# Loading q and k with 48 rows instead of 40, the last eight zeros

## The chip, the cores and the metric

The kernel runs on one core of a Trainium2 chip. The metric is device time in microseconds of one execution; several executions are timed and the median is given. The engines of the core are TensorE (PE, with its weight loads shown as PEld), VectorE (DVE), ScalarE (ACT), GpSimd (POOL) and SyncE (SP), which here issues nearly all DMA transfers. Sixteen DMA engines carry the transfers.

## What is computed

An mLSTM recurrence over 4 batches, 8 heads and 768 tokens with a head dimension of 40, gated and normalized, and then a dense layer of 3072 tokens: 320 to 2048, softplus, 2048 to 320.

```python
for t in range(S):
    m_new = np.maximum(f_gate[:, :, t] + m, i_gate[:, :, t])
    f_stab = np.exp(f_gate[:, :, t] + m - m_new)
    i_stab = np.exp(i_gate[:, :, t] - m_new)
    C = f_stab[:, :, None, None] * C + i_stab[:, :, None, None] * np.einsum('bhd,bhe->bhde', vt, kt)
    n = f_stab[:, :, None] * n + i_stab[:, :, None] * kt
    h_tilde = np.einsum('bhde,bhe->bhd', C, qt)
    denom = np.maximum(np.abs(np.einsum('bhd,bhd->bh', n, qt)[:, :, None]), 1.0)
    y[:, :, t] = o * h_tilde / denom
x = y.transpose(0, 2, 1, 3).reshape(B * S, H * D)
h = x @ w_in
g = np.maximum(h, 0.0) + np.log1p(np.exp(-np.abs(h)))
out = g @ w_out
```

## The kernel before

The recurrence is cut into 24 steps of one batch and 128 tokens each. A step has its scores (products of k and q, 64 tokens by 64, `scores`, L463), the decay matrix that weighs them (`decay`, `by_decays`), the products of k and decayed v for the state (`states`, L480), the values (`values`, L579 and L587, or `values_wide`, L640 and L652), and then normalization, gate and transpose into a tile X (`turn_x`, L707 and L709). Three steps make a group of 384 tokens, eight groups in all. The dense layer runs group by group in 16 blocks of 128 hidden units: eight products into hp (L974), softplus, nine products into po (L937). The matmuls of the dense layer fill TensorE; the steps of later groups are worked into the gaps between the blocks. Only the first group has nothing to run beside it: its three steps, and the splitting of the first weights, come before the first product of L974.

q and k of a step are loaded by `load` (L382): one tile `qk` of 128 partitions, three buffers, with the head dimension on the partitions, 1024 floats (q and k, four heads, 128 tokens) a row. The heads come in two halves (x is 0 or 1): one half goes to the partitions from 0, the other to those from 64 (PP is 64). Each half is one transfer, issued on SP; the third transfer of `load` is `vt`, v and k by token, with 128 rows. D is 40, EP is 48. The products read rows `x * PP` to `x * PP + D` and no others.

The order of all work is written out by hand: `WHEN` gives a time for each piece, and `in_order` fixes the order of the instructions on each engine. SP's order at the start is: gates, first weights, q/k and vt of step 0, q/k and vt of step 1, output gates, q/k and vt of step 2, a write of gate values, more weights. In the first 40 us TensorE's order is: warm-up products on `po1` (L731), gate spreading, decay broadcasts of steps 0 and 1 (L396), scores of step 0, decay broadcast of step 2 (L396), scores of step 1, states of step 0, warm-up, values of step 0, warm-up, states of step 1, values of step 1, scores, states and values of step 2, the transposes, scores and states of step 3, first product. Tiles of the scores are named ga, or po for step 1, whose scores lie in spare banks; those of the values gc, or po.

Of the kernel before, what the change touches and what calls it, by code (L numbers as in the profile page):

```python
# [17 lines left out]
B, H, S, D = 4, 8, 768, 40  # L18
# [14 lines left out]
PP = 64  # L33
EP = 48
# [8 lines left out]
def mlstm_moe_kernel(  # L43
# [11 lines left out]
    nc = tc.nc  # L55
# [322 lines left out]
    def load(z):  # L378

        z.qk = p2.tile([128, 2, HG, L], F32, tag="qk", bufs=3, name=f"qk{z.n}")  # L380
        for x in range(2):
            nc.sync.dma_start(z.qk[x * PP : x * PP + D], qk[z.s, x])  # L382
        z.q, z.k = z.qk[:, 0], z.qk[:, 1]
        z.vt = p2.tile([128, VW + DM], F32, tag="vt", bufs=3, name=f"vt{z.n}")
        nc.sync.dma_start(z.vt, vk[z.s])
        z.v1 = z.vt[:, 0:VW].rearrange("p (q j e) -> p q j e", q=NQ, j=HG)
        z.kt = z.vt[:, VW:]
# [443 lines left out]
    def plain_step(z, times):  # L831
        spare = z.s in (1, 2)
        fs = dict(
            load=load, fb=decays, scan=decay, vi=gate_values, vw=state_values, sig=out_gate,
            ga=plain_scores, pm=by_decays, st=states, cp=keep_states, old=decay_old,
            mid=mid_state, new=new_state, gc=lambda z: values(z, z.s in SPARE_C), sum=sum_values, nrm=norm, sg=scale_gate, x=gated,
            xp=turn_x, xh=high_x, xl=low_x,
        )
        for (name, f), t in zip(fs.items(), times, strict=True):
            once(f"{name}{z.s}", t, event, name, f, z)  # L840
# [3 lines left out]
    def wide_step(z, base, after):  # L844
        d = 18 + 30 * (z.s == NH)
        g = after - base
        for name, f, t in (
            ("fb", decays, -64), ("load", load, -48), ("scan", decay, -8), ("vw", state_values, 2), ("old", decay_old, 6),
            ("ga", group, 14), ("pm", by_decays, 17), ("cp", keep_states, 17), ("vi", gate_values, 20), ("mid", mid_state, 24),
            ("new", new_state, 30), ("fc", load_decays, g - 34),  # L850
        ) + ((("gc", values_wide, g),) if z.s == NS - 1 else ()) + (
            ("ym", scale_wide, g + 5), ("ya", add_wide, g + 5), ("yd", write_wide, g + 8), ("rd", read_wide, g + 42),
            ("fin", finish_wide, g + 91 + d), ("end", end_wide, g + 92 + d), ("xh", high_wide, g + 95 + d),
            ("xl", low_wide, g + 98 + d),
        ):
            once(f"{name}{z.s}" if z.s < 9 else name, base + t, event, name, f, z, base=base)
# [328 lines left out]
```

## Time and profile before

| | us |
|---|---|
| median of three runs | 439.82 |
| lowest and highest | 436.81, 440.22 |
| span of the profiled execution | 438.4 |

| engine | busy us | share of the span |
|---|---|---|
| PE | 427.3 | 97% |
| DVE | 253.6 | 58% |
| ACT | 214.5 | 49% |
| POOL | 106.1 | 24% |

The profile is of one execution. Busy time of PE is that of pipelined matmuls. The granted clock is given as a share: 1.00 is 2.4 GHz, 0.50 is 1.2 GHz. The DMA share is the mean over the sixteen DMA engines. The DMAs moved 55.93 MB in the span. The chain that ended last is 95% PE and 3% DMA.

### The profile page before, as it was taken

Reading aid. Unit: us, or ns where it says so; the run is one execution under the profiler, and the core shown is the slowest. Engines: PE = TensorE matmul, PEld = TensorE weight load, DVE = VectorE, ACT = ScalarE, POOL = GpSimd, SP = SyncE. Lnnn points to the kernel's source line nnn. Section 1 sums busy time; section 2 is a strip of 40 time slices with the busy share of each in tenths; the row PEclk is TensorE's granted clock in tenths of the full one; section 3 lists DMA queues with packets and bytes.
Section 4 is the critical chain, followed back from the end, with each engine's and each line's share of the span. In section 5 each row is a group of like instructions: output and inputs, shape, how many; then the busy total and the mean of one; then the engine's idle time right before and its main releaser. Section 6 shows DMA issues by size and latency. Waiting matters only on the chain.

```text
span 438.4 us, 12718 instructions
## 1 busy us (share of the span) xinstructions
PE 427.3 (97%) x5302; PEld 414.3 (95%) x5302; DVE 253.6 (58%) x479; ACT 214.5 (49%) x445; POOL 106.1 (24%) x171
## 2 busy tenths in 40 slices
PE   7869999999999999999999999999999999999997
PEld 6758999999999999999999999999999999999996
DVE  6678998677866556456465556466365554422221
ACT  5388898768347333534236333544336333333332
POOL 3425334545454302111132202121122200000000
PEclk9568999999999999999999999999999999999999
DMA  7877886776376373544463263553553331001001
GB/s 197 263 218 206 234 256 178 222 197 182 82 171 182 95 192 75 135 125 104 116 179 107 59 163 94 151 125 84 135 164 88 99 95 36 0 1 46 1 0 46
DMA packets 52089, 55.93 MB, mean 128 GB/s; under 512 B 5664, under 2 KB 42176, under 8 KB 52032
## 3 DMA queue, kind: packets, MB, share of 16 engines
q1 hardware_dynamic: 49008, 51.68, 43.1%
q10 hardware_dynamic: 3024, 3.44, 2.3%
q8 instruction: 41, 0.67, 0.6%
q14 instruction: 16, 0.13, 0.1%
HBM read 46.47 MB, written 8.64 MB: 126 GB/s over the span
## 4 chain that ended last, share of the span: by engine, by line
PE 95%; DMA 3%; issue 1%; ACT 0%; DVE 0%; SPq 0%
PE hp L974 41%; PE po L937 40%; PE ga L463 3%; PE gc L652 2%; PE gc L640 2%; PE ga L480 2%; PE po L731 2%; DMA qk<-in_qk 2%; DMA wr<-in_w_in 1%; PE xp L709 1%; PE gc L579 1%; PE gc L587 1%; PE xp L707 1%; PE gb L463 1%; PE gb L480 0%
## 5 line engine op out<-in xcount | busy, mean ns | idle before, releaser
L974 PE MATMUL hp<-X,wih 128*128 128x384 f32 x768 | 175.3, 337 | 0.0
L862 ACT ACTIVATE gh<-hp 128x384 fp32r<-128x384 f32 x128 | 63.0, 492 | 168.0 <-PE hp L974 140.6
L866 DVE TENSOR_TENSOR gl<-hp,gh 128x384 fp32r<-128x384 f32 x128 | 70.7, 555 | 123.1 <-ACT hp L863 122.8
L974 PEld LDWEIGHTS hp<-X,wih 128*128 128x128 f32 x768 | 133.3, 188 | 0.3 <-issue 0.2
L937 PE MATMUL po<-woh,gl 128*128 128x320 f32 x384 | 83.2, 313 | 0.0
L937 PE MATMUL po<-woh,gh 128*128 128x320 f32 x384 | 80.7, 310 | 0.0
L937 PE MATMUL po<-wol,gh 128*128 128x320 f32 x384 | 80.7, 310 | 0.0
L937 PEld LDWEIGHTS po<-woh,gh 128*128 128x128 f32 x384 | 65.8, 188 | 0.2
L974 PE MATMUL hp<-X,wil 128*128 128x384 f32 x256 | 65.7, 337 | 0.0
L937 PEld LDWEIGHTS po<-woh,gl 128*128 128x128 f32 x384 | 62.3, 188 | 0.9 <-issue 0.2
L937 PEld LDWEIGHTS po<-wol,gh 128*128 128x128 f32 x384 | 62.1, 188 | 0.8 <-issue 0.3
L863 ACT ACTIVATE hp<-hp 128x384 f32<-128x384 f32 x128 | 62.4, 487 | 0.0
L974 PEld LDWEIGHTS hp<-X,wil 128*128 128x128 f32 x256 | 46.1, 188 | 0.1
L426 POOL TENSOR_TENSOR vw<-vt,gw 128x328 f32<-128x328 f32 x22 | 17.4, 790 | 118.4 <-DVE gw L417 105.3
L412 DVE TENSOR_TENSOR_SCAN pw<-fb,ident 128x512 f32<-128x512 f32 x24 | 30.1, 1256 | 0.0
L426 POOL TENSOR_TENSOR values_in<-vt,gT 128x328 f32<-128x328 f32 x18 | 13.3, 739 | 67.7 <-PE gc L652 63.9
L463 PEld LDWEIGHTS ga<-qk 40*64 40x64 f32 x448 | 13.2, 134 | 5.5 <-issue 3.9
L558 POOL TENSOR_TENSOR c<-c,cp 104x164 f32<-104x164 f32 x20 | 14.1, 703 | 15.0 <-DVE c L426 13.7
L463 PE MATMUL ga<-qk 40*64 40x64 f32 x448 | 16.6, 224 | 1.1 <-DMA qk<-in_qk 1.1
L685 DVE RECIPROCAL nm<-nm 128x128 f32<-128x128 f32 x18 | 17.2, 953 | 0.6
L480 PE MATMUL ga<-vw,vt 64*40 64x41 f32 (+1 forms) x416 | 14.2, 222 | 2.3 <-issue 2.3
L426 POOL TENSOR_TENSOR c<-c,flast 104x164 f32<-104x164 f32 x33 | 15.6, 473 | 1.0
(159 smaller groups left out, 477.6 us busy)
## 6 DMA issues: line engine op xcount, KB each, us to landing
vt<-in_vk SPq DMA_DIRECT2D x24, 324.0 KB
qk<-in_qk SPq DMA_DIRECT2D x48, 160.0 KB
fb<-fz_d SPq DMA_DIRECT2D x42, 128.0 KB
wo<-in_w_out SPq DMA_DIRECT2D x8, 640.0 KB
wr<-in_w_in SPq DMA_DIRECT2D x8, 512.0 KB
eg<-in_oT SPq DMA_DIRECT2D x6, 576.0 KB
yd<-y SPq DMA_DIRECT2D x36, 96.0 KB
out<-ob ACTq DMA_DIRECT2D x21, 160.0 KB
```

The lines of the kernel that those rows point to most:

```text
L412: nc.vector.tensor_tensor_scan(z.pw.rearrange(flat), z.fb.rearrange(flat), ident4.rearrange(flat), 0.0, ALU.mult, ALU.add)
L426: e.tensor_tensor(to, of, by.unsqueeze(3).broadcast_to([to.shape[0], a, b, w]), op=ALU.mult)
L463: nc.tensor.matmul(z.ga[x][y * Q : (y + 1) * Q, (i * NQ + q) * Q : (i * NQ + q + 1) * Q], z.k[rows, g, ts], z.q[rows, g, ts], start=True, ...
L480: nc.tensor.matmul(z.ga[y][x * PP : x * PP + w, c0 : c0 + E], z.kt[y * Q : (y + 1) * Q, j * D : j * D + w], z.vw[y * Q : (y + 1) * Q, q, x ...
L558: nc.gpsimd.tensor_tensor(heads(c), heads(c), z.cp[:, :, 1], op=ALU.add)
L640: nc.tensor.matmul(gc[out, x, c0 : c0 + Q], (z.cm if q else z.old)[rows, g * E : g * E + w], z.q[rows, g, q * Q : (q + 1) * Q], start=True ...
L685: nc.vector.reciprocal(nm, nm)
L862: nc.scalar.activation(gh, hp, AF.Softplus)
L863: nc.scalar.activation(hp, hp, AF.Softplus)
L866: nc.vector.tensor_tensor(gl, hp, gh, op=ALU.subtract)
L937: nc.tensor.matmul(po[j], a[:, j * 128 : (j + 1) * 128], w[:, f, :], start=(first and left[j] == 2), stop=(last and left[j] == 0),)
L974: nc.tensor.matmul(hp, a, r, start=(i == 0), stop=(i == len(seq) - 1))
```

## The change

Each of the two transfers that load a step's q and k takes 48 rows instead of 40. The array in the chip's memory is made with 48 rows a half, the last eight of zeros, when the inputs are laid out. So partitions 40 to 47 and 104 to 111 of the tile, which nothing wrote before, now receive zeros. No product reads them, and no other line is changed.

```diff
         z.qk = p2.tile([128, 2, HG, L], F32, tag="qk", bufs=3, name=f"qk{z.n}")
         for x in range(2):
-            nc.sync.dma_start(z.qk[x * PP : x * PP + D], qk[z.s, x])
+            nc.sync.dma_start(z.qk[x * PP : x * PP + EP], qk[z.s, x])
@@
         [np.stack([by_bits(a, b, c).transpose(2, 4, 1, 0, 3).reshape(2, D, HG, L) for a in (q, k)], axis=2) for b, c in ORDER]
     )
+    qk = np.concatenate([qk, np.zeros(qk.shape[:2] + (EP - D,) + qk.shape[3:], np.float32)], axis=2)
```

## Rows read from the trace of the kernel before

**Rows 1.** Busy us (and count) of each engine by stretch, granted clock, DMA share, GB/s.

```profile
0.00:40.00 40.00, 32.20 (x547) 27.48 (x548) 28.00 (x65) 24.24 (x42) 16.59 (x34) 0.74 0.76 221
40.00:430.00 390.00, 389.97 (x4723) 382.03 (x4724) 224.55 (x413) 188.51 (x399) 89.55 (x137) 1.00 0.44 119
```

**Rows 2.** Timeline of PE: start, us, line, operands, count, idle before and releaser.

```profile
8.51 0.33 PE L463 MATMUL ga<-qk 40*64 40x64 f32 x2 [0.41 <-DMA qk<-in_qk]
9.51 0.69 PE L463 MATMUL ga<-qk 40*64 40x64 f32 x30 [0.68 <-DMA qk<-in_qk]
10.13 1.09 PE L396 MATMUL fb<-g,ident 128*64 128x128 f32 x16
11.60 0.32 PE L463 MATMUL po<-qk 40*64 40x64 f32 x2 [0.38 <-DMA qk<-in_qk]
12.75 1.02 PE L463 MATMUL po<-qk 40*64 40x64 f32 x27 [0.83 <-DMA qk<-in_qk]
```

**Rows 3.** The chain that ended last, in order of time: start, us, what.

```profile
5.77 6.94 DMA qk<-in_qk
...
13.88 0.80 PE ga L480 x23
...
22.05 0.80 PE po L480 x20
...
24.97 2.35 issue
...
32.18 0.62 PE xp L707 x2
...
35.44 0.43 PE xp L707 x2
...
37.37 1.59 PE hp L974 x8
```

**Rows 4.** Timeline of DVE, columns as in rows 2.

```profile
24.60 0.50 DVE L426 TENSOR_TENSOR y1z<-po,fcT 64x328 f32<-64x328 f32 x1 [2.37 <-PE po L587]
...
26.53 0.68 DVE L493 TENSOR_TENSOR pw<-ga,pw 128x512 f32<-128x512 f32 x1
```

**Rows 5.** Busy time by stretch, columns as in rows 1.

```profile
12.10:22.30 10.20, 9.27 (x146) 8.37 (x150) 6.27 (x12) 3.52 (x5) 4.21 (x6) 0.50 0.84 269
...
25.70:36.00 10.30, 8.08 (x104) 6.23 (x106) 9.14 (x21) 9.18 (x15) 4.95 (x6) 0.50 0.57 156
```

**Rows 6.** DMA packets, then issues: tile, queue, count, KB each.

```profile
DMA packets 52089, 55.93 MB, mean 128 GB/s; under 512 B 5664, under 2 KB 42176, under 8 KB 52032
...
vt<-in_vk SPq DMA_DIRECT2D x24, 324.0 KB
qk<-in_qk SPq DMA_DIRECT2D x48, 160.0 KB
...
y<-fc_d SPq DMA_DIRECT2D x18, 96.0 KB
...
flast<-fl_d SPq DMA_DIRECT2D x4, 24.0 KB
...
fl_d<-fl_s SPq DMA_DIRECT2D x2, 0.8 KB
...
fz_d<-g SPq DMA_DIRECT2D x1, 16.0 KB
```

**Rows 7.** Busy time by stretch, columns as in rows 1.

```profile
5.00:10.00 5.00, 3.88 (x77) 3.18 (x75) 3.92 (x11) 2.56 (x4) 1.40 (x2) 1.00 0.93 246
10.00:15.00 5.00, 3.79 (x96) 3.27 (x87) 4.96 (x7) 0.63 (x1) 4.07 (x5) 0.71 0.90 250
...
17.00:18.00 1.00, 1.00 (x6) 0.89 (x5) 0.00 (x0) 0.98 (x2) 0.25 (x1) 0.50 1.06 401
```

**Rows 8.** Timeline of SP's queue: start, us, line, transfer, count.

```profile
3.96 0.74 SPq L382 DMA_DIRECT2D qk<-in_qk  x2
4.74 0.36 SPq L385 DMA_DIRECT2D vt<-in_vk  x1
5.14 0.91 SPq L382 DMA_DIRECT2D qk<-in_qk  x2
```

## The prediction

> **What bounds the kernel now.** I read the busy time by stretch first, then TensorE's waits and clock in the first 40 us, then the chain that ended last, then the transfers.
>
> By stretch, TensorE stands idle 7.80 us in the first 40 us and 0.03 us in the 390 us after that [rows 1]. From 40 us on a transfer that lands earlier or later changes nothing unless it is late by its whole reserve, because TensorE has no gap to lose. So the 48 loads that the change touches (24 steps, two each) are not worth 48 times something; only the loads of the first steps can move the end. What they can move is the moment at which the first big product starts, 37.3 us.
>
> In the first 13 us TensorE waits four times for q and k: 0.41 and 0.68 us for the two halves of step 0, 0.38 and 0.83 us for those of step 1, 2.30 us together, or a third of its idle time there [rows 2]. The first two don't sit on the path that sets the end: what follows them (the decay broadcast at 10.13 us) is over before step 1's q and k are there. The last one does: the chain of waits runs through this load for 6.94 us until 12.71 us and from there only through work [rows 3]. The reader should see there that TensorE goes on without another transfer up to 24.97 us, then stands for 2.35 us, and reaches the first product at 37.37 us. The 2.35 us are no transfer: the state products of step 2 write the bank that VectorE still reads (26.53 us plus 0.68 is 27.21, TensorE goes on at 27.32), and VectorE's own run began at 24.60 us, when step 1's values were finished [rows 4]. So the chain goes TensorE, VectorE, TensorE, and whatever moves the 12.71 us moves it as a whole.
>
> The clock: granted 0.50 (1.2 GHz) from 12.1 to 22.3 us and again from 25.7 to 36.0 us [rows 5], both after stretches in which TensorE had stood still part of the time; after that it is 1.00 (2.4 GHz).
>
> **The change, step by step.**
>
> *Does a load get more engines?* The count of small packets answers it. The 30 rows of issues, from the vt row to the last fz_d row, add up to 352 transfers. Of the 5664 packets under 512 bytes, 256 are data of flast (4 transfers of 64 rows of 384 bytes) and 64 are data of fl_d (2 transfers of 32 rows of 24 bytes). That leaves 5344. Sixteen small packets for each transfer would be 5632, so 288 are missing: exactly 6 for each of the 48 q/k loads [rows 6]. So a load of 40 rows runs on 10 of the 16 DMA engines, 4 rows each, and every other transfer, the 18 y loads of 48 rows (96 KB) among them, runs on 16. With 48 rows I expect 16 engines with 3 rows each. In bytes a load grows by 8 rows, 32 KB or 20%; on the engines that finish last it shrinks by one row, 25%.
>
> *What one row costs.* An engine's rate while these loads are under way: 246 GB/s at a busy share of 0.93 of 16 engines is 16.5 GB/s, 250 at 0.90 is 17.4; the best stretch, 401 GB/s at 1.06, gives 23.6 [rows 7]. A row of 4096 bytes takes 0.25, 0.24 or 0.17 us.
>
> *What moves.* Ahead of the second half of step 1's load stand three other halves (issued from 3.96 and from 5.14 us, in order) [rows 8], all on the same 10 engines; the four give back a row each, so it lands 4 rows earlier: 0.94 to 0.99 us at the stretch's own rates, 0.69 us at the best one. The other transfers keep their share per engine. I take 0.9 us, near the stretch's own rate. Step 0's second half gains two rows, 0.5 us, so the decay broadcast that follows is over at about 10.8 us instead of 11.2 and doesn't stand in the way of a start at 11.85 us.
>
> *What follows it down the chain.* From 12.75 us on the pieces wait for each other, so they all come 0.9 us earlier. But if the clock rises at 22.3 and 36.0 us as before, work slides from 2.4 to 1.2 GHz: step 1's state products (0.80 us on the chain for 20 pieces, mostly after 22.3) go back to step 0's rate at half clock (0.80 us for 23, with the rest run in among other work): I take 0.1 us. The transposes of step 2 at 35.44 us (two of 0.43) go back to 0.62 each: 0.4 us [rows 3]. That gives back 0.5 us in the worst case, and nothing where the clock changes elsewhere. Net gain 0.4 to 0.9 us; I take 0.5, because the clock's changes stand where I read them in the only execution that I have.
>
> *Costs taken at nothing.* Issue on SP: the two q/k halves take 0.74 us, the vt load with 128 rows takes 0.36, so rows don't set the issue time [rows 8]; if they did, 20% of 0.74 is 0.15 us on a queue whose transfers lie microseconds ahead. The 1.57 MB of zeros (384 rows) are hidden in 390 us with a DMA share of 0.44 [rows 1]; without that cover they would cost 1.57 MB at 246 GB/s, 6.4 us. The eight more partitions are read by nobody: the products take 40 rows as before. The tile's buffers come free at the same times. What SP issues behind these loads (step 2's loads, weights) can go out earlier too, but on the chain after 12.71 us no piece is a transfer [rows 3], so I count nothing.
>
> **Rivals.**
>
> *A. The clock doesn't fall at 12.1 us.* With 0.9 us less waiting TensorE may look busy enough. For it: in the stretch before the fall TensorE had stood idle mainly for q and k. Price: 9.27 us of TensorE work between 12.1 and 22.3 us ran at 0.50 [rows 5], at 1.00 it takes 4.6 us; ScalarE work in between (the copies of the states) takes some of it back, so 4 us less in all, together with the forecast 4.5. Against it: the clock also fell at 25.7 us, after a stand of VectorE's making that stays. The Trainium skill (TensorE: Matmul & The Clock Gate, Part 1: The HAM clock gate) says that the gate follows how busy the engine has been recently; the trace agrees in that both falls come after partly idle stretches. Chance 0.12.
>
> *B. Bytes, not rows per engine, set the landing.* All 16 engines are busy at 0.93 in the stretch, since the six that carry no q and k run ahead with later transfers; if what limits is shared, four loads of 32 KB more at 246 GB/s come 0.5 us later: end 0.5 us later at most. Against it: if it is shared, the six engines' running ahead also takes from it, and that stops. [...] Here belongs also the case that the change doesn't do what it says: were 48 rows spread over 12 engines, each would carry four rows as now, and the time would stay as it is; the y loads of 48 rows speak against it [rows 6]. Chance 0.2.
>
> *C. Slower by over 1%.* The clock falls once more, or rises after the first product has begun. Place: after 36 us, where all work is TensorE's. Price: a spell as long as the two here, 10.2 us at half speed, costs 5.1 us. It decides when the clock still stands at 0.50 after 37 us. For it: the rise of 36.0 us comes only 1.4 us before the first product, and the forecast draws the product nearer. Against it: TensorE is then busy without a gap, as in all of the 390 us. Chance 0.05.
>
> **How the numbers follow.** The execution in the profile has a span of 438.4 us; the median of the three runs, 439.82, lies 1.4 us above, and the runs reach from 436.81 to 440.22. I take the middle between span and median, 439.1 us, less 0.5: 438.6 us. Chances: forecast 0.6, A 0.12, B 0.2, C 0.05, anything else 0.03. The range: below, the fastest run before less 0.9 is 435.9, and A reaches 434.6, so 435.4 leaves out the far half of A; above, the slowest run plus B's 0.5 is 440.7. A measurement of this kernel tells about 1% (4.4 us) from no change. Only A with a fast run gets there, and C on the other side: faster 0.09, same 0.87, slower 0.04.
>
> **What would show it.** Packets under 512 bytes 5952 (352 times 16, plus 320), packets in all 52761 (384 rows and 288 small ones more), 57.5 MB. The second half of step 1's scores starts at about 11.85 us; TensorE's waits for q and k fall from 2.3 to 1.0 to 1.5 us; the first product starts between 36.4 and 36.9 us; idle from 40 to 430 us stays below 0.1 us. Wrong would be: step 1's scores at 12.7 us or later (B), a granted clock of 1.00 between 12 and 22 us (A), or 0.50 after 37 us (C).

## The result and the profile after

The kernel after takes 441.04 us in the median (438.75 to 444.55), the kernel before 439.0 (435.25 to 441.98), 20 executions of each. The ratio is 1.0067, with a 95% interval of 1.0040 to 1.0094: slower by 2.9 us. The medians are 2.0 us apart, the means of all executions 2.9 us, as the ratio says. That is within the 1% that the prediction called no change, but it is on the other side of the forecast, and the median lies above the range. The profiled execution of after has a span of 437.2 us.

From the page of after: the granted clock in 40 slices, the packets, and the queue that brings the instructions.

```profile
PEclk9959999999999999999999999999999999999999
...
DMA packets 52761, 57.50 MB, mean 132 GB/s; under 512 B 5952, under 2 KB 42464, under 8 KB 52704
...
q8 instruction: 41, 0.67, 0.6%
```

The packets are those that were forecast, so the loads do run on 16 engines [rows 6]. Queue q8 is new to the argument: the program itself comes by DMA, in 41 pieces of 16 KB. TensorE has 10,604 instructions (5302 products, 5302 weight loads on the page), 259 for each piece if all the pieces are TensorE's. The queue doesn't name the engine that a piece is for.

Busy time of after by stretch, columns as in rows 1.

```profile
0.00:40.00 40.00, 32.19 (x605) 27.20 (x606) 30.84 (x69) 26.92 (x47) 17.86 (x37) 0.87 0.86 245
40.00:430.00 390.00, 388.55 (x4674) 380.61 (x4673) 222.07 (x409) 186.03 (x396) 88.73 (x134) 1.00 0.46 121
5.00:10.00 5.00, 4.26 (x79) 3.59 (x79) 3.81 (x11) 2.56 (x4) 1.40 (x2) 1.00 0.99 221
10.00:15.00 5.00, 3.65 (x89) 3.04 (x90) 4.96 (x7) 1.45 (x3) 4.00 (x5) 1.00 1.07 268
12.10:22.30 10.20, 7.49 (x241) 6.58 (x241) 7.93 (x15) 6.23 (x15) 5.03 (x7) 1.00 0.91 274
23.10:33.40 10.30, 8.95 (x122) 6.78 (x126) 8.66 (x20) 9.71 (x15) 5.79 (x7) 0.50 0.98 295
```

Two things changed. Between 40 and 430 us TensorE now stands 1.45 us where it stood 0.03 [rows 1]. And the clock took another course: it stayed at 1.00 (2.4 GHz) through the stretch in which it had been at 0.50 [rows 5], and fell to 0.50 (1.2 GHz) once, from 23.1 to 33.4 us, instead of twice. Ahead of that fall TensorE had been busy for 7.49 of 10.2 us.

Timeline of TensorE after, columns as in rows 2: the q and k waits, then the stands after them.

```profile
9.28 0.69 PE L463 MATMUL ga<-qk 40*64 40x64 f32 x30 [0.74 <-DMA qk<-in_qk]
9.89 1.09 PE L396 MATMUL fb<-g,ident 128*64 128x128 f32 x16
11.43 0.32 PE L463 MATMUL po<-qk 40*64 40x64 f32 x2 [0.45 <-DMA qk<-in_qk]
12.38 0.63 PE L463 MATMUL po<-qk 40*64 40x64 f32 x27 [0.62 <-DMA qk<-in_qk]
...
17.32 0.33 PE L587 MATMUL gc<-vi,pw 64*64 64x41 f32 x8 [0.79 <-issue]
...
22.51 0.27 PE L463 MATMUL ga<-qk 40*64 40x64 f32 x1 [1.01 <-issue]
...
94.09 0.27 PE L463 MATMUL gb<-qk 40*64 40x64 f32 x1 [1.04 <-DVE gl L866]
...
97.21 0.62 PE L974 MATMUL hp<-X,wih 128*128 128x384 f32 x2 [0.41 <-DVE gl L866]
```

The second half of step 1 starts at 12.38 us instead of 12.75 [rows 2], 0.37 us earlier. That is one profile of each, and other runs, told of below, undo it. The second half in late48b, which has 40 rows here, then in rows48 and rows48b, which are the change once more (columns as in rows 2):

```profile
12.73 0.63 PE L464 MATMUL po<-qk 40*64 40x64 f32 x27 [0.56 <-DMA qk<-in_qk]
```

```profile
12.35 1.02 PE L463 MATMUL po<-qk 40*64 40x64 f32 x27 [0.16 <-DMA qk<-in_qk]
```

```profile
13.17 0.63 PE L463 MATMUL po<-qk 40*64 40x64 f32 x27 [0.66 <-DMA qk<-in_qk]
```

It starts at 12.17 to 12.75 us in the five profiles with 40 rows in the first nine steps (before, rows40, pad40, late48, late48b), and at 12.09 to 13.17 us in four with 48 rows in the front (after, rows48, rows48b, front48): 12.5 us in the mean of either. So nothing was gained.

Behind it TensorE has stands that before did not have. The one at 22.51 us is none of the change's: late48b has it too.

```profile
21.78 0.27 PE L464 MATMUL ga<-qk 40*64 40x64 f32 x1 [0.94 <-issue]
```

A stand released by issue between 20 and 24 us is found in eight of the nine profiles whose clock stays at 1.00 from 12 to 23 us, with 40 rows (late48, late48b, shift40) as with 48, and in none of the nine others; it goes with the course of the clock. The stand of 1.04 us goes back through VectorE to ScalarE, which waited for a weight load. ScalarE's waits from 80 to 95 us, after and then before (what waited, for what: us in total, times, longest):

```profile
ACT mago L253 <- DMA wo<-in_w_out: 5.6, 1, 5.6
```

```profile
ACT mago L253 <- DMA wo<-in_w_out: 3.1, 1, 3.1
```

The softplus of the products is queued behind that wait, VectorE waits for the softplus, and TensorE for VectorE.

### The profile page after: what moved, and what is told of

Its sections match the earlier page's. It is cut to its first block, busy times and chain, and to the rows that moved or that the text cites. A ratio compares the mean times of both kernels' runs of the same rounds, so it can differ in the third digit from the quotient of the medians.

```text
span 437.2 us, 12718 instructions
## 1 busy us (share of the span) xinstructions
PE 424.7 (97%) x5302; PEld 411.5 (94%) x5302; DVE 254.0 (58%) x479; ACT 214.2 (49%) x445; POOL 106.6 (24%) x171
## 4 chain that ended last, share of the span: by engine, by line
PE 94%; DMA 2%; ACT 1%; SPq 1%; issue 1%; DVE 0%; ACTq 0%
PE hp L974 41%; PE po L937 39%; PE ga L463 2%; DMA qk<-in_qk 2%; PE gc L652 2%; PE gc L640 2%; PE ga L480 2%; PE po L731 1%; PE xp L709 1%; PE xp L707 1%; PE gc L587 1%; PE gb L463 1%; PE gc L579 1%; PE gb L480 0%; PE pg L137 0%
## 5 line engine op out<-in xcount | busy, mean ns | idle before, releaser
L558 POOL TENSOR_TENSOR c<-c,cp 104x164 f32<-104x164 f32 x20 | 14.0, 701 | 15.0 <-DVE c L426 13.7
L549 POOL TENSOR_TENSOR c<-c,cp 104x164 f32<-104x164 f32 x20 | 13.1, 656 | 9.0 <-ACT cp L762 7.3
```

What stands on the lines that cost most here:

```text
L549: nc.gpsimd.tensor_tensor(heads(z.cm), heads(z.cm), z.cp[:, :, 0], op=ALU.add)
L558: nc.gpsimd.tensor_tensor(heads(c), heads(c), z.cp[:, :, 1], op=ALU.add)
```

## The experiments

One figure sorts all that follows. In each profile I read three numbers: where the first big product starts, how long TensorE stands after it (gaps of 0.1 us and more), and the span. Span less the other two is 401.0 to 402.1 us in every kernel but two (mid42 and mid48, 403.0 and 403.3, where the clock also fell once more behind 61 us). So each profile's span is told by the first product and by the stands behind it. The last column is the one found out last: when one piece of instructions starts on its way, seen from the first score product of the step at about 95 us.

| kernel | q/k loads of the first 97 us | first product | stands after it | span | piece, from that step |
|---|---|---|---|---|---|
| before | 40 rows, 10 engines | 37.30 | 0.00 | 438.4 | -0.53 |
| rows40 (before again) | 40, 10 engines | 37.34 | 0.00 | 438.3 | -0.43 |
| pad40 | 40, 10 engines | 36.65 | 0.00 | 437.7 | -0.68 |
| late48 | 40, 10 engines | 33.89 | 0.19 | 435.3 | -1.03 |
| late48b | 40, 10 engines | 32.75 | 0.40 | 434.6 | -0.60 |
| mid50 | 50 in steps 3 to 8, 10 engines | 37.13 | 0.00 | 438.2 | -1.04 |
| rows50 | 50, 10 engines | 39.79 | 0.87 | 442.7 | +0.69 |
| front48 | 48 in steps 0 to 2, 16 engines | 36.28 | 0.79 | 438.7 | +0.82 |
| shift40 (before, with the shift told below) | 40, 10 engines | 33.42 | 0.00 | 434.4 | -4.37 |
| after | 48, 16 engines | 34.19 | 1.45 | 437.2 | +0.85 |
| rows48 | 48, 16 engines | 36.65 | 1.00 | 438.8 | +0.59 |
| rows48b | 48, 16 engines | 34.98 | 2.69 | 439.0 | +0.63 |
| shift48 (after, with that shift) | 48, 16 engines | 34.23 | 0.57 | 436.6 | +0.05 |
| rows45 | 45, 15 engines | 37.05 | 1.44 | 440.6 | +0.73 |
| rows42 | 42, 14 engines | 32.54 | 2.33 | 436.4 | +2.10 |
| mid48 | 48 in steps 3 to 8, 16 engines | 32.07 | 4.92 | 440.3 | +1.17 |
| mid42 | 42 in steps 3 to 8, 14 engines | 32.56 | 3.40 | 439.0 | +0.24 |
| mid32 | 32 and 8 apart in steps 3 to 8 | 36.31 | 1.14 | 439.3 | +0.33 |

The first product swings by 5 us with the course of the clock, in kernels of either kind, so one profile says little of the median. The stands don't swing that way: 0 to 0.4 us where the early loads go to ten engines with four rows each, or with five in steps 3 to 8 alone; 0.6 to 4.9 us everywhere else. The last column parts the same two groups. So does a count that leaves TensorE's stands out: the same piece, the tenth, starts 0.0 to 1.4 us after TensorE's 2451st instruction in the first group, and 2.1 to 4.4 us after it in the second (2.7 in after).

**Other numbers of rows.** The same edit with another count; 45 rows use 15 engines, 42 use 14, and 50 use 10 with five rows each (packets under 512 bytes: 5904, 5856, 5664, by the same sum as in the prediction). rows48 is the change once more.

```diff
-    qk = np.concatenate([qk, np.zeros(qk.shape[:2] + (EP - D,) + qk.shape[3:], np.float32)], axis=2)
+    qk = np.concatenate([qk, np.zeros(qk.shape[:2] + (ROWS - D,) + qk.shape[3:], np.float32)], axis=2)
-            nc.sync.dma_start(z.qk[x * PP : x * PP + EP], qk[z.s, x])
+            nc.sync.dma_start(z.qk[x * PP : x * PP + ROWS], qk[z.s, x])
```

> 45 rows a load, five of zeros. If 45 rows run on 15 DMA engines with three rows each, packets under 512 bytes become 352 times 16, plus 320, less 48: 5904. Theory 1 (instruction blocks): TensorE's instruction blocks of 16 KB come on one DMA engine that the 40-row loads leave free; with 48 rows that engine has q and k too, the first block starts at 14.5 us instead of 11.3 and TensorE stands about 1 us twice between instructions that wait for nothing. If that engine is the last of the sixteen, 45 rows leave it free: the first block comes before 12 us again, no such stand, and q and k land as early as with 48: as fast as the kernel before or up to 1 us faster. If it is another one, 45 rows are like 48: about 3 us slower. Theory 2 (bytes): 12.5% more bytes of q and k instead of 20%: about 60% of the loss, 1.8 us slower than the kernel before.

> 42 rows a load, two of zeros. On 14 DMA engines with three rows each packets under 512 bytes are 5952 less 96: 5856. Theory 1 (instruction blocks): if the engine that brings TensorE's instruction blocks is one of the last two, the first block comes before 12 us, TensorE has no stand between instructions in the first 25 us, and the time is that of the kernel before or up to 1 us less; if it is among the other fourteen, about 3 us slower, as with 48 rows. Theory 2 (bytes): 5% more bytes, a quarter of the loss, 0.7 us slower.

> 50 rows a load, ten of zeros: on 10 DMA engines with five rows each packets under 512 bytes stay 5664. Theory 1 (instruction blocks): the last six engines stay free, the first instruction block starts before 12 us as before, no stand between instructions; q and k land later, by a row each, four rows or about 1 us at step 1, so up to 1.5 us slower than the kernel before. Theory 2 (bytes): 25% more bytes of q and k, so slower than with 48 rows: 3.5 us or more.

> The change itself again, for a second profile and for times on the same chip as the other sizes. Both theories: 3 us (0.7%) slower than the kernel before. Theory 1: the first instruction block starts after 13.5 us, and TensorE stands between instructions that wait for nothing in the first 25 us, 1 us or more in all. Theory 2: no such stand is needed; step 2's loads and the weights land 1 us or more later than before.

Ratios to before: 45 rows 1.0043 (1.0013 to 1.0073), 42 rows 1.0047 (1.0011 to 1.0083), 50 rows 1.0121 (1.0083 to 1.016), 48 rows 1.0054 (1.0021 to 1.0088). Forty-two rows have only 5% more bytes than 40 and lose about as much as 45 or 48, so the loss doesn't go by bytes, as far as intervals of this width tell. Fifty rows lose most, on ten engines. Every load of the front is a row longer there on its ten engines, TensorE's waits for q and k of steps 0 and 1 are 1.24, 1.03 and 0.38 us, the clock stands at 0.50 from 11.6 to 38.9 us without a rise in between, and the first product comes at 39.79 us.

**Where in the run.** 48 rows in some steps only, in an array of 48 rows; rows40 is the kernel before once more.

```diff
-            nc.sync.dma_start(z.qk[x * PP : x * PP + EP], qk[z.s, x])
+            w = EP if 3 <= z.s < 9 else D      # mid48; front48: z.s < 3, late48: z.s >= 9
+            nc.sync.dma_start(z.qk[x * PP : x * PP + w], qk[z.s, x, 0:w])
```

> 48 rows only in the loads of steps 0 to 2 (issued in the first 11 us), 40 rows in the other 21 steps; small packets 5664 plus 36, 5700. Theory 1 (instruction blocks of TensorE held back in the first 30 us): the whole loss or most of it, 2 to 3 us slower than the kernel before. Theory 2 (more bytes and more engines reading at once delay the weights that the first 100 us need): a small part, 0 to 0.8 us slower (6 loads of 32 KB at 240 GB/s are 0.8 us).

> 48 rows only in the loads of steps 3 to 8 (issued from 19 to 90 us), 40 rows in the other steps; small packets 5664 plus 72, 5736. Theory 1: no loss, the first 19 us are those of the kernel before. Theory 2: most of the loss, 1.5 to 2.5 us slower; ScalarE waits 4 us or more for w_out at 85 to 95 us (3.1 before) and TensorE stands 0.5 to 2 us between 60 and 100 us.

> 48 rows only in the loads of steps 9 to 23 (issued from 97 us on), 40 rows in the first nine; small packets 5664 plus 180, 5844. Both theories: no loss, within 0.5 us of the kernel before, since TensorE has no gap after 100 us. A loss of 1 us or more here would fell both.

> The kernel before once more, for a second profile. Theory 1: the first two instruction blocks of TensorE start less than 2.5 us after the kernel after's do relative to its work, no stand between instructions in the first 25 us. Theory 2: TensorE stands less than 0.5 us between 60 and 100 us, and ScalarE's wait for w_out at about 85 to 95 us is under 4 us.

front48 1.0012 (0.9978 to 1.0046), mid48 1.0035 (1.0001 to 1.0069), late48 0.9956 (0.9928 to 0.9984), rows40 0.9966 (0.9917 to 1.0014). From 97 us on the longer loads cost nothing that shows; in steps 3 to 8 they measured 1.5 us more, with an interval that hardly leaves out no change, and rows40, the kernel before itself, measured 1.5 us less. front48 can't be told from nothing. Theory 1 of the expectations, that late pieces of instructions in the front make the loss, did not hold: rows48 has no stand released by issue in the first 25 us and is slower all the same, and pad40 and mid50, with 40 rows in the front, get their first piece at 13.4 and 13.9 us like rows48 (13.9), without the loss. Waits in mid48, DVE's from 54 to 62 us, then TensorE's from 40 to 110 us, columns as above:

```profile
DVE pw L413 <- DMA fb<-fz_d: 3.4, 1, 3.4
```

```profile
PE ga L464 <- issue: 3.2, 1, 3.2
PE po L938 <- issue: 1.3, 1, 1.3
```

The first goes with a late load: the forget gates of a step land at 57.8 us, VectorE waits for them 3.4 us, and TensorE stands 3.2 until VectorE has worked off what lay behind that wait. The profile names no releaser for it; that TensorE waits for VectorE there is read from the order of the two. In the kernel before the same load is waited for by nobody. The second, 1.3 us, comes with no late transfer of data and no late engine. It is the stand that the last group of experiments is about.

late48's gain needed a second look, because the loads that matter by every other run are those of before there.

> The 48 rows from step 9 on alone, once more. If its 0.44% gain is one of the kernel: 0.994 to 0.997 of the kernel before. If it was chance: within 0.2% of it. Either theory of the loss: not slower than before, with no stand near 97 us.

late48b measured 1.0007 (0.9973 to 1.0041): the gain of 0.44% did not come back. So the interval of late48 promised more than it held, as a dozen executions over several courses of the clock can, and no single ratio here carries a conclusion of 0.4% by itself; the profiles have to agree with it.

**Layout, bytes or engines.** pad40 keeps the array of 48 rows and loads 40 of them. mid50 adds 25% of bytes in steps 3 to 8 on the same ten engines. mid42 adds 5% on 14 engines. mid32 adds none: from the kernel before, each load of steps 3 to 8 is issued as 32 rows (16 engines) and 8 rows (8 engines).

```diff
-            nc.sync.dma_start(z.qk[x * PP : x * PP + D], qk[z.s, x])
+            for w in ((0, 32), (32, D)) if 3 <= z.s < 9 else ((0, D),):
+                nc.sync.dma_start(z.qk[x * PP + w[0] : x * PP + w[1]], qk[z.s, x, w[0] : w[1]])
```

> The array of q and k has 48 rows as in the change, but every load takes 40 of them, so the transfers have before's sizes and engines and only the distance in memory from one load's rows to the next is the change's. Either theory of traffic: the time of the kernel before, within 0.4%. If the distance alone matters: it moves either way by the 0.4% that the kernel with 48 rows from step 9 on gained, or by the 0.5 to 0.7% that the change lost.

> The kernel before with its own bytes, but each load of q and k of steps 3 to 8 issued as two, 32 rows and 8 rows; 32 rows go to 16 engines, 8 rows to 8. No byte more than before. Bytes as the cause: the time of the kernel before. Spread over all engines as the cause: the loss of the kernel with 48 rows in steps 3 to 8, +1.5 us, with the weight and forget-gate loads between 50 and 90 us landing 1 to 3 us later than before and TensorE idle by 0.5 to 3 us between 55 and 100 us. SP issues 12 transfers more, some 0.7 us of its time by its issues of before, spread over steps.

> 42 rows in the loads of steps 3 to 8 alone: 5% more bytes in them, on 14 engines in place of 10. Bytes as the cause: a quarter of the loss with 48 rows there, +0.4 us, not to be told from nothing. Spread as the cause: +1 to 1.5 us.

> 50 rows in the loads of steps 3 to 8 alone: 25% more bytes in them than before, on the same 10 engines, five rows on each. Bytes as the cause: 1.25 times the loss with 48 rows there or more, +2 us. Spread as the cause: the time of the kernel before.

pad40 0.9981 (0.9948 to 1.0015): the layout does no harm. mid32 1.0043 (1.0013 to 1.0072): the kernel before, not a byte more, loses 1.9 us. mid42 and mid50 1.0017 each (0.9981 to 1.0054, 0.9979 to 1.0054): undecided by the time. The profiles tell more than the times. TensorE's waits from 40 to 110 us in mid32 hold one line:

```profile
PE gc L653 <- issue: 1.1, 1, 1.1
```

In mid50 and pad40 there is none. In mid42 there are 2.7 and 0.6 us, the pair of mid48. ScalarE's longest wait for a wo load from 40 to 100 us is 2.3 to 3.5 us in before, rows40, pad40, late48, late48b, mid50 and shift40, and 3.9 to 5.6 us in all the others but rows48b, where it is 1.9 and a wait of 3.8 us for VectorE, itself held up by a late fb load, stands beside it. So mid32 lost time without a byte more, and 25% more bytes on the same engines did not bring the stands. That is for the spread, but it isn't proof. mid32 also issues 12 transfers more: SP takes 1.51 us for a step's q and k at 84 us where before takes 0.72, not the 0.7 us in all that was expected, so its 1.9 us may not be the spread's alone. And the long waits for wo aren't all a slow wo load: from its issue near 80 to 87 us until ScalarE goes on, it takes 5.6 to 7.1 us in the seven kernels with short waits and 7.3 to 8.8 in nine others, but 6.6 and 6.7 in rows48 and mid32. In front48 and rows50 it takes 8.8 and 8.7 us, with the loads beside it on ten engines.

**The piece of instructions.** What does TensorE wait for when it waits for nothing that the profile shows? Busy time of rows48 by stretch, columns as in rows 1: the products ahead of the step, and the step.

```profile
95.20:97.34 2.14, 2.14 (x129) 2.00 (x128) 0.84 (x4) 2.14 (x5) 0.05 (x1) 1.00 0.26 64
92.80:94.94 2.14, 2.14 (x15) 2.14 (x14) 0.85 (x2) 2.14 (x5) 0.42 (x1) 1.00 1.02 239
```

A step's small products run through 257 instructions in 2.14 us, where big products take 29. That is a whole piece of 259 in 2 us, and behind it TensorE stands 1.00 us in rows48:

```profile
96.69 0.64 PE L652 MATMUL gc<-pw,values_in 64*48 64x64 f32 x29
98.33 0.71 PE L937 MATMUL po<-woh,gl 128*128 128x320 f32 x3 [1.00 <-issue]
```

The trace has a piece of instructions under way from 95.79 to 96.95 us there, 0.59 us behind the step's first product; in before it starts 0.53 us ahead of it, and there is no stand. If TensorE is out of instructions, moving its instructions against the borders of the pieces must take the stand away, with the transfers left as they are. So the eight broadcast products of the third step's gate are issued twice, in the front, between two waits for q and k (in the trace 16 products and 16 weight loads, 32 instructions more), in the change and in before.

```diff
-            for j in range(HG):
+            for j in [*range(HG)] * (2 if z.s == 2 else 1):
```

> The change, with the eight broadcast products of the third step's forget gate (line 396) issued twice, in the front where TensorE waits for q and k anyway: 16 products and 16 weight loads more in TensorE's stream, so every later instruction sits 32 places further in its instruction blocks. Theory of the instruction block (the stand of about 1.0 to 1.3 us behind the dense products of the step at 95 us, released by issue alone, is TensorE out of instructions, since the block asked for at about 95 us came over 1 us late): the stand is gone, and the time is lower than that of the change by about 1 us. Rival (the stand is the late work of VectorE, ScalarE or a transfer): the stand and the time stay as with the change.

> The same 16 products more in the kernel before: the price of the addition by itself. Both theories: the time of the kernel before, with 0 to 1 us on top where the added 1.1 us of products is not covered by the waits for q and k at 10 to 12.8 us; no stand behind the dense products at 95 us. If the kernel before too loses at its block boundaries, other than at 95 us, it moves by that.

> The change once more, on the chip of these runs, to stand beside the others: 1.005 to 1.007 of the kernel before by either theory, with a stand of 0.4 to 1.3 us near 97 us.

Medians 438.64, 436.88 and 440.92 us beside 437.22 of before; ratios 1.0026 (0.9993 to 1.006), 0.9975 (0.9949 to 1.0001) and 1.0069 (1.0032 to 1.0105). TensorE's stand at that step, in rows48b and in shift48 (columns as in rows 2):

```profile
98.52 0.71 PE L937 MATMUL po<-woh,gl 128*128 128x320 f32 x3 [1.08 <-issue]
```

```profile
95.68 0.45 PE L652 MATMUL gc<-pw,values_in 64*64 64x64 f32 x16 [0.17 <-issue]
```

In shift40 there is none. The stand shrank from 1.08 to 0.17 us and the median by 2.3. Not all of that is the stand: the added products also steadied the clock (12 of 12 executions of shift40 have a mean clock of 0.987 or more, 10 of 12 of shift48, 20 of 35 of before, 6 of 12 of rows48b). Among the executions with 0.987 or more the medians are 436.26 us for before, 436.89 for shift40, 438.82 for rows48b and 438.47 for shift48. So 48 rows cost 2.56 us without the shift and 1.58 with it. The 0.98 us between them is what the theory of the piece said, but the times don't show it: there are 20, 12, 6 and 10 executions, drawing them anew at random gives a 95% interval of -0.2 to 2.1 us, and the same sorting puts rows40, the kernel before itself, 2.65 us below before. One profile with 0.17 us doesn't settle it either: after, without the shift, has no such stand at this step, where TensorE stood 1.04 us for VectorE while the piece was on its way, and front48 and rows45 have 0.18 and 0.41. The better evidence is when such stands end, told below. The rest of the loss remains.

The piece itself is late in the change. Queue q8 in shift40 from 87.5 to 87.7 us, and in shift48 from 92.7 to 92.9 us (packets that start there, MB, share of the engines):

```profile
q8 instruction: 1, 0.02, 41.1%
```

```profile
q8 instruction: 1, 0.02, 45.7%
```

It is the same piece of the same program, and TensorE is only 0.8 us later in shift48 (step's first product at 92.76 and 91.96 us); the piece starts 5.2 us later. The 32 instructions of reserve nearly hold: 0.17 us are left.

Stands released by issue end alike: twenty of them in thirteen kernels end 1.2 to 1.7 us after the transfer of a piece has ended (after at 17.32 and 22.51 us, rows48 at 98.33, rows48b at 23.24 and 98.52, shift40 at 20.84, shift48 at 16.55, 22.59 and 95.68, one near 16 us in mid48, one near 22 us in late48, late48b, rows42 and mid42, and one each behind 94 us in front48, rows45, rows42, mid32, mid42 and mid48). So the two in the front of after, 0.79 and 1.01 us, look to be of this kind too, and late48, late48b and shift40 show that 40 rows have them as well. Stands of 1.27 to 2.35 us at 22 to 30 us (in before the one that the prediction puts down to VectorE) and near 60 us don't end so. In the three longest near 60 us (mid48, mid42, rows48b) VectorE waited 3.4, 2.9 and 1.6 us for the fb load.

## Why the prediction was wrong

**The engines** were right: 10 before, 16 after, by the small packets to the unit. The Trainium skill (DMA: Bandwidth & Descriptors, Why a DMA increments its semaphore by 16 and not by 1) says that a transfer issued from SP runs on the largest number of engines, up to 16, that divides the slowest dimension of both its sides; the counts with 40, 42, 45, 48 and 50 rows agree, 10, 14, 15, 16 and 10.

**The price of a row** was taken as fixed, 0.17 to 0.25 us, and four rows fewer as 0.9 us. This is the step that failed first: with 48 rows a row takes longer. In the first 14 us a row of 4096 bytes was under way for 203 to 216 ns in the mean in the five profiles with 40 rows (before, rows40, pad40, late48, late48b) and for 241 to 330 ns in the four with 48 (after, rows48, rows48b, front48). Four rows at the one price and three at the other are the same 0.8 us, so of the 0.9 us nothing is left. The engines were busier and moved no more: from 5 to 15 us their share was 1.00 to 1.05 for 229 to 260 GB/s in five profiles with 48 rows there, and 0.90 to 0.94 for 239 to 279 GB/s in ten with 40. That fits the mechanism of rival B, a limit that all share; its time, 0.5 us later, was not met either. Whether the engines or the rows make the price isn't told apart: in rows50, with five rows on each of ten engines, a row of the first 14 us took 265 ns. One reading of the prediction was off without harm: 2.30 us are over half of the 4.0 us that TensorE stands in the first 13 us, not a third.

**Issue on SP**, taken at nothing because "rows don't set the issue time", was mis-sized by a little. SP's queue in after, columns as in rows 8:

```profile
3.96 0.89 SPq L382 DMA_DIRECT2D qk<-in_qk  x2
4.89 0.43 SPq L385 DMA_DIRECT2D vt<-in_vk  x1
5.37 0.89 SPq L382 DMA_DIRECT2D qk<-in_qk  x2
```

Step 0's two loads take 0.89 us instead of 0.74 [rows 8], and the next step's first load goes out at 5.37 us instead of 5.14. With 50 rows on ten engines they take 0.73 us and with 42 on 14 engines 0.84, so for these loads the time went with the number of engines and, as the prediction said, not with the rows. It is 0.2 us of the gain that was forecast.

**"What SP issues behind these loads … I count nothing"** and **the zeros that "are hidden in 390 us"** are the steps on which, as far as the runs show it, the sign turned: stands of 1.0 to 2.7 us behind the first product in the three profiles of the change, 0 to 0.4 us in those with 40 rows. Whether the bytes of the zeros have a part in it stays open. The reason given was that the chain held no transfer behind 12.71 us [rows 3] and that a DMA share of 0.44 leaves room [rows 1]. The first is one execution's chain, the second a mean. The share from 40 to 430 us is low because the later part of the run moves little; up to 100 us it is 0.68 to 0.82 in each 20 us of before. And a transfer that is not on the chain still has a finite reserve, which I named ("unless it is late by its whole reserve") and did not work out: the wo load of 80 us was already late by 3.1 us for ScalarE in before, and the piece of instructions at 95 us came 0.53 us ahead of the step that used it up. Both were on the edge, and TensorE's forecast idle of under 0.1 us behind 40 us became 1.45. The chain of after now has two waits behind 12.71 us that the forecast ruled out, a stand and the load of step 2 (start, us, what):

```profile
16.52 0.79 issue
...
20.23 3.59 DMA qk<-in_qk
```

**The clock.** Rival A happened in the profiled execution, and the first product started at 34.19 us, 3.1 us earlier, 0.9 to 1.4 short of A's price. It is no doing of the change: late48, late48b and shift40, with 40 rows in the front, have one fall too, and of before's 35 executions beside shift40, 20 have a mean clock of 0.987 or more, like the profiles with one fall (after 0.987, shift40 and rows48b 0.988; pad40, with two, has 0.977). The forecast's chain was one of the kernel's courses, and a chain that moves as a whole, less what the clock takes back, can't be seen against a swing of 5 us. Nothing of rival C showed in after. mid48 showed its mechanism: behind the stand of 3.2 us the clock was 0.50 once more, from 61.0 to 64.4 us.

**The sum as the runs give it.** Among executions of a like mean clock 48 rows cost 2.56 us, roughly. Stands behind the first product are 1.45, 1.00 and 2.69 us in the three profiles of the change, 1.7 in the mean, against 0 to 0.4 with 40 rows on ten engines. The first product gives no clear term. With a mean clock of 0.87 in the first 40 us it starts at 34.19, 34.23 and 34.98 us with 48 rows, and at 33.89 and 33.42 with 40 in the first steps: 0.8 us later. But with a mean clock of 0.79 it starts at 36.28 and 36.65 us with 48 rows (front48, rows48), and at 36.31 and 37.13 with 40 (mid32, mid50): 0.3 us earlier. So the stands are about two thirds of the loss, and no run shows where the rest is.

**What stays open.** What makes the other transfers and the pieces of instructions late. The spread over more engines fits mid32, mid42 and mid48, and mid50 speaks against bytes; but no run shows on which engine a piece travels, and two kernels have the late piece and the late wo load with ten engines beside them: front48, with 40-row loads from step 3 on, and rows50. Whether bytes have a part: mid50's interval leaves room for 2.4 us, its profile shows no stand.

## What to carry to other kernels

Before a transfer is made wider, list who else lives on those engines and how far ahead of its use each arrives. Work that runs out of reserve first decides, and it may be weights, gates or the program itself. A rule such as the one to use all 16 engines (the Trainium skill, DMA: Bandwidth & Descriptors, Rules for kernel authors) is about one transfer alone; here 40 rows on ten engines were better than 42, 45 or 48 on 14, 15 or 16, and than 50 on ten. The transfer that was made wider came no earlier, and its neighbours had reserve to lose. Stands "released by issue" behind a stretch of very many short instructions are worth a look at the instruction queue; some instructions more in a place where the engine waits anyway can move the border.

## What the runs showed of the hardware

- Instructions come by DMA in pieces of 16 KB among the data, each 0.9 to 1.9 us under way in the first 100 us. TensorE ran through a whole piece in about 2 us in a dense step, and in twenty stands released by issue it went on 1.2 to 1.7 us after a piece's transfer had ended.
- Sixteen engines under these loads moved no more than the mix of ten and six: 229 to 260 GB/s against 239 to 279 from 5 to 15 us, with 241 to 330 ns a row against 203 to 216 in the first 14 us.
- SP took 0.73 us to issue step 0's two q/k loads where they ran on ten engines (40 or 50 rows), 0.84 on 14, 0.87 on 15 and 0.89 on 16; one vt load on 16 engines behind them took 0.36 to 0.43.
- The same program takes more than one course of the clock, and the first big product moves with it: 32.75 to 37.3 us in kernels whose first 97 us have the same loads. With eight broadcast products issued twice between two waits, 12 of 12 executions had a mean clock of 0.987 or more, against 20 of 35. No kernel here beats both for certain: shift40's 0.9975 (0.9949 to 1.0001) is not told from no change.
